# Context matmuls out of the shared two-bank PSUM tile, and its two banks given back one by one

## The chip, the cores and the metric

The kernel runs on one core of a Trainium2 chip. The metric is the device time of one execution in microseconds (us), the median over several runs. Five engines work side by side, each through its own queue in program order: TensorE (PE, matrix products; its weight loads are PEld in the profile), VectorE (DVE), ScalarE (ACT), GpSimd (POOL) and SyncE (SP), which here issues the loads and stores. PSUM, where PE writes its results, has eight banks; a bank takes 512 float32 values on each of the 128 partitions.

## The reference, cut to what matters

Three stages follow one another. The first is chunked attention over 2 x 8 heads, 768 positions and head size 64; the second a mixture of 4 experts without a gate (each expert's result is weighted by normalised probabilities); the third one more pair of products with a leaky activation.

```python
# attention, for each chunk of 32 queries; 8 memory keys, up to 16 keys to the left and 8 to the right
scores = scale * np.matmul(q_c, k_full.transpose(0, 1, 3, 2))
a = np.exp(scores - np.max(scores, axis=-1, keepdims=True))
out[:, :, c_start:c_end] = np.matmul(a / (np.sum(a, axis=-1, keepdims=True) + 1e-09), v_full)
# experts: x is 1536 x 512, w1[e] 512 x 1024, w2[e] 1024 x 512
for e in range(E):
    out += p[:, e:e + 1] * (np.maximum(x @ w1[e], 0.0) @ w2[e])
# last stage: w_in 512 x 2048, w_out 2048 x 512
h = x @ w_in
return (np.maximum(h, 0.0) + alpha * np.minimum(h, 0.0)) @ w_out
```

## The kernel before

**Attention.** The 12 units of 128 queries are cut into 24 half-units (`half_unit`, four heads each). A half-unit has five steps that other work may be put between. Scores: 16 small products, two heads `e` by two pairs of heads `z` by four windows `w` of 32 queries; each takes 64 rows (the head's dimension, so the two `e` use the upper and the lower half of the array) and writes 32 partitions, 64 keys wide. VectorE takes the maximum and subtracts it, ScalarE takes the exponent, two transposes (`t_ps`) put keys on the partitions and ScalarE copies them to `pt`. Context: again 16 small products, 64 rows (the keys of one head) into 32 partitions, 65 wide: 64 values and a column of ones that gives the sum. VectorE adds 1e-9, takes the reciprocal and scales into `xs`; two transposes (`xt_ps`) and a ScalarE copy put the result into `acc`.

Scores and context lie in one PSUM tile, `two`, of two banks (bank `e` for head `e`). Within it the scores of even and odd half-units have columns of their own (`s0`), and the context a third stretch of columns. `load_half` brings a half-unit's queries and keys, `load_v` its values (one transfer, 128 partitions of 2080 bytes in a row) into rings of four half-units (RING, RINGV). Each load is issued by SP behind the products that last read its buffer.

**The order of the work.** The program's order is fixed when it is built, by a model clock `now`: each product adds its planned time (T_S, T_X, T_T, or 13 ns + n/2.4 ns in `mm`), and polls put attention steps, weight preparation (`prep_w`: high and low parts on ScalarE and GpSimd or VectorE) and the conversion of the last stage's weights (`convert`) between the products where the clock says they are due. `Pinned` keeps every engine's instructions in this order. The first 12 half-units run in `att_cycle`: scores of half-unit m, final transposes of m-3, context of m-2, exponent of m, a few filler products (`keep_warm`), transposes of m-1. The other 12 are put between the products of the first tile.

**The products.** The rest is 48 tiles (24 planes of 256 hidden columns by two halves of the columns). `gemm1` is a fast 2x2 block product: seven products a, b, d, a, c, d, c of six matmuls, 384 columns each, in four PSUM banks that VectorE and ScalarE read between them (`add`, `gelu`). `gemm2` is eight results `y` of six matmuls, each read by `evac` when it is complete (VectorE adds it to `acc`). From the third tile on the order is gemm1 of tile k, then gemm2 of tile k-1; only around the change from experts to the last stage (k = 30 to 33) does it differ, since the last stage's input must be complete.

**Banks.** `bank()` hands out PSUM for everything but scores and context. Until the third tile (k = k0 = 2) there are six single banks, tag `ps`. From there on `freed` is set: two of each eight calls get the two halves of a newly allocated two-bank tile, also tagged `two`, and the other six get single banks. A tile takes four calls in gemm1 and eight in gemm2, so the pair falls on d and c of gemm1 in every second tile and on two neighbouring y in every tile. In the profile a product into the pair is named after the call that allocated it, `two_d` (both d and c) or `two_y`.

Almost every instruction of the kernel goes through `Pinned`, and so has line 60; rows are told apart by the tiles' names.

Of the kernel before, what the change touches and what calls it, by code (L numbers as in the profile page):

```python
# [21 lines left out]
WIN = CH  # L22
# [9 lines left out]
P = 128  # L32
# [33 lines left out]
def tile_kernel(ctx: ExitStack, tc: tile.TileContext, qk, v, wa, wq, dpt, alpha, out):  # L66
# [5 lines left out]
    xp = ctx.enter_context(tc.tile_pool(name="xp", bufs=1))  # L72
    bp = ctx.enter_context(tc.tile_pool(name="bp", bufs=1))
    dp = ctx.enter_context(tc.tile_pool(name="dp", bufs=1, space=bass.MemoryType.DRAM))
    ps = ctx.enter_context(tc.tile_pool(name="ps", bufs=1, space=bass.MemoryType.PSUM))
    two = ps.tile([P, 2, 512], F32, tag="two", name="two")
    taken, freed = [0], []

    def bank(name):
        taken[0] += 1  # L80
        if freed and taken[0] % 8 < 2:
            if len(freed) == 1:
                freed.append(ps.tile([P, 2, 512], F32, tag="two", name=f"two_{name}"))
                return freed[1][:, 0]
            return freed.pop()[:, 1]
        return ps.tile([P, 512], F32, tag="ps", bufs=6, name=name)


    ident = cp.tile([P, P], F32, name="ident")
    make_identity(nc, ident)  # L90
# [53 lines left out]
    def keep_warm(hu):  # L144

        o = bank(f"keep{hu}")[:, :NCOL // 2]
        now[0] += 0.1
        for i in range(5 if hu < 6 else 4):
            mm(o, xh[:, 10 + i % 4, NCOL // 2:NCOL // 2 + P], xh[:, 13, spare], n=NCOL // 2, start=True, stop=True)

    def prep_x(c0, n, fast):
# [34 lines left out]
    def mm(*a, n, took=None, **kw):  # L186
        pe_.matmul(*a, **kw)
        now[0] += took or 0.013 + n / 2.4e3


    qk_t = [bp.tile([P, QW + KW], F32, tag="ggB", bufs=4, name=f"qk{i}") for i in range(RING)]
    v_t = [bp.tile([P, 2, NW, VW], F32, tag="w2", bufs=4, name=f"v{i}") for i in range(RINGV // 2)]
    pe_ring = bp.tile([P, 2, HP, 2, KEYS], F32, tag="ft", bufs=3, name="pe_ring")
    pt_ring = bp.tile([P, 2, HP, BLK], F32, tag="fr", name="pt_ring")
    xs_ring = bp.tile([P, 2, HP, 2, D], F32, tag="ft", bufs=3, name="xs_ring")
# [6 lines left out]
    def load_v(hu):  # L202
        if hu >= 2 * NU:
            return
        dst = v_t[hu % RINGV // 2][:, hu % 2].rearrange("p w f -> p (w f)")
        sync.dma_start(dst, v[hu // 2, :, hu % 2])

    def half_unit(u, half):

        hu = 2 * u + half  # L210
        qv = qk_t[hu % RING][:, :QW].rearrange("p (z q) -> p z q", q=BLK)
        kv = qk_t[hu % RING][:, QW:].rearrange("p (z k) -> p z k", k=SPAN)
        vv = v_t[hu % RINGV // 2][:, hu % 2].rearrange("p w (z d) -> p w z d", d=D + 1)
        c, ab = divmod(u, 2)
        cols = slice(c * BLK, (c + 1) * BLK)
        hs = slice(2 * half, 2 * half + 2)
        nm = f"{u}_{half}"

        def tiles():
            now[0] += T_SW  # L220
            for z in range(HP):
                for w in range(NW):
                    for e in range(2):
                        yield z, w, e, slice(w * WIN, (w + 1) * WIN), slice(e * D, (e + 1) * D)

        s0 = hu % 2 * HP * KEYS
        s_ps = two[:, :, s0:s0 + HP * KEYS].rearrange("p e (z k) -> p e z k", k=KEYS)
        for z, w, e, r, rows in tiles():
            mm(s_ps[r, e, z], qv[rows, z, r], kv[rows, z, w * STEP:w * STEP + KEYS], n=KEYS, took=T_S,
               start=True, stop=True)  # L230
        load_half(hu + RING)
        mx = cp.tile([P, 2, HP], F32, tag="mx", bufs=4, name=f"mx{nm}")
        dve.tensor_reduce(out=mx, in_=s_ps, axis=AX.X, op=ALU.max)
        pe = pe_ring[:, hu % 2]
        dve.tensor_tensor(
            out=pe.rearrange("p z e k -> p e z k"), in0=s_ps,
            in1=mx.unsqueeze(3).to_broadcast([P, 2, HP, KEYS]), op=ALU.subtract,
        )
        yield LATE
        act.activation(pe, pe, AF.Exp, scale=scale)  # L240
        yield LAT[0]
        t_ps = bank(f"t{nm}")[:, :HP * BLK].rearrange("p (z q) -> p z q", q=BLK)
        now[0] += T_SW
        for z in range(HP):
            pe_.transpose(t_ps[:, z], pe[:, z].rearrange("p e k -> p (e k)"), ident)
            now[0] += T_T
        pt = pt_ring[:, hu % 2]
        act.copy(pt, t_ps)
        yield LAT[1]
        x_ps = two[:, :, 2 * HP * KEYS:2 * HP * KEYS + VW].rearrange("p e (z d) -> p e z d", d=D + 1)  # L250
        for z, w, e, r, rows in tiles():
            mm(x_ps[r, e, z], pt[rows, z, r], vv[rows, w, z], n=D + 1, took=T_X, start=True, stop=True)
        load_v(hu + RINGV)
        dn = cp.tile([P, 2, HP, 1], F32, tag="dn", bufs=2, name=f"dn{nm}")
        dve.tensor_scalar_add(dn, x_ps[:, :, :, D:D + 1], 1e-9)
        rd = cp.tile([P, 2, HP, 1], F32, tag="rd", bufs=2, name=f"rd{nm}")
        dve.reciprocal(rd, dn)
        xs = xs_ring[:, hu % 2]
        dve.tensor_tensor(out=xs.rearrange("p z e d -> p e z d"), in0=x_ps[:, :, :, :D],
                          in1=rd.to_broadcast([P, 2, HP, D]), op=ALU.mult)  # L260
        yield LAT[2]
        xt_ps = bank(f"xt{nm}")[:, :2 * BLK].rearrange("p (c q) -> p c q", q=BLK)
        now[0] += T_SW
        for z in range(HP):
            pe_.transpose(xt_ps[:, z], xs[:, z].rearrange("p e d -> p (e d)"), ident)
            now[0] += T_T
        act.copy(acc[:, hs, ab, cols], xt_ps)
        if ab == 1 and half == 1:
            while att["x"] < c:
                yield 0.2  # L270
            for _ in prep_x(c * BLK, BLK, c in FAST):
                yield X_STEP[c]
            att["x"] = c + 1
# [339 lines left out]
    def gemm2(p, c0, n, gs, soon, last):  # L613
        prep_force("w", lambda: p in w2)
        wh, wl = w2[p]
        y = {}

        def part(o, ab, i, start, stop, z0=0, z1=n):
            lag_poll(lambda: 2 * i + ab in gs)
            gh, gl = gs[2 * i + ab]  # L620
            if start:
                y[o, ab] = bank(f"y{p}_{c0}_{o}_{ab}_{z0}")[:, :n]
            w_ = [x[:, 2 * i + o // 2, (o % 2) * P:(o % 2 + 1) * P] for x in (wh, wl)]
            for k, (a, b) in enumerate(((w_[0], gh), (w_[1], gh), (w_[0], gl))):
                product(y[o, ab][:, z0:z1], a, b[:, z0:z1], n=z1 - z0,
                        start=start and k == 0, stop=stop and k == 2)
            if stop:
                evac(p, c0 + z0, z1 - z0, o, ab, y[o, ab][:, z0:z1])

        if soon:  # L630

            for o in range(4):
                part(o, 0, 0, True, False)
            for o in range(2):
                part(o, 1, 1, True, False)
            for o in range(4):
                part(o, 0, 1, False, True)
            for o in range(2):
                part(o, 1, 0, False, True)
        else:  # L640
            for o in range(4):
                part(o, 0, 0, True, False)
                part(o, 0, 1, False, True)
            for o in range(2):
                part(o, 1, 1, True, False)
                part(o, 1, 0, False, True)
        for o in range(2, 4):

            end = p == NP - 1 and c0 + n == NCOL and o == 3
            for z0, z1 in ((0, n // 2), (n // 2, n)) if end else ((0, n),):  # L650
                part(o, 1, 1, True, False, z0, z1)
                part(o, 1, 0, False, True, z0, z1)
        if last:
            used2.add(p)
# [27 lines left out]
        order += [(1, k), (2, k - 1)]  # L682
    order += [(2, len(tiles) - 1)]

    for i in range(3):
        load_half(i)
        load_v(i)
    stream("w", weights())
    streams["w"][0] = PREP0
    acts = {}  # L690
    gated = []
    begun = [
        (1, lambda: load_half(3)),
        (1, lambda: load_v(3)),
        (1, lambda: load_raw(0, 0)),
        (2, lambda: sync.dma_start(praw, dpt.rearrange("e (p i) -> p e i", i=NI))),
        (6, lambda: sync.dma_start(nalpha, alpha)),
# [1 line left out]
    for i, (what, k) in enumerate(order):  # L699
        p, c0, n = tiles[k]  # L700
        if k == k0 and what == 1:
            freed.append(None)
            dve.tensor_scalar_mul(nalpha, nalpha, -1.0)
        if what == 1:
            if p == 0:
                while att["done"] < 4 * -(-(c0 + n) // BLK):
# [7 lines left out]
                    if att["done"] >= 3 and not gated:  # L714
                        gated.append(gate())
                        begun.append((11, lambda: load_pb(0, *FIRST[0])))
                        begun.append((12, lambda: load_raw(0, 1)))
            if k == k0:
                stream("c", convert())
                streams["c"][0] = now[0] + 20.0  # L720
# [17 lines left out]

LAT = (1.0, 0.8, 1.6)
LATE = 1.3  # L740
T_S, T_X, T_T, T_SW = 0.016, 0.016, 0.11, 0.1
FAST = (1, 2, 5)
LIVE = 4
PACE = 1.9
PACE0 = 2.0
X_STEP = (1.2, 0.8, 0.4, 1.0, 1.0, 0.4)
PREP0 = 6.0

# [4 lines left out]
T_CONV = 18.0  # L753
DT_X = 0.35
RING = 4
RINGV = 4
WARM = 18


# [72 lines left out]
```

## Time and profile before

| what | value |
|---|---|
| median of 3 runs | 970.69 us (964.85, 970.69, 971.05) |
| the profiled execution's own time | 965.82 us |
| its span, from the first to the last instruction | 964.0 us |
| mean granted TensorE clock, as a share of full speed | 0.985 |

The profile shows one execution. Busy times of engines are unions of their instructions' times; a matmul's start to its end is longer than the distance to the next, because matmuls are pipelined. An idle time is written in brackets behind the instruction that it precedes, with what ended it.

### The profile page before, as it was taken

How to read it: one execution, taken by the hardware profiler on the slowest of the kernel's cores; microseconds unless marked ns; L12 is line 12 of the kernel's file. 1: busy time of each engine (PE TensorE's matmuls, PEld its weight loads, DVE VectorE, ACT ScalarE, POOL GpSimd, SP SyncE). 2: the span in 40 equal slices, each digit the busy share in tenths (PEclk: the TensorE clock that was granted, in tenths of full speed). 3: DMA queues.
4: the chain of work that ended last, by engine and by line, in shares of the span. 5: the costliest groups of instructions: out<-in, count | busy, mean ns of one | idle time of the engine just before them, and what ended most of it. 6: DMA issues, size and time to landing. Idle time of an engine off the chain costs nothing. (4 is left out here: it accounts for less than half of the span.)

```text
span 964.0 us, 15786 instructions
## 1 busy us (share of the span) xinstructions
PE 849.5 (88%) x6046; PEld 798.7 (83%) x6046; DVE 593.4 (62%) x1157; ACT 338.6 (35%) x754; POOL 567.1 (59%) x604
## 2 busy tenths in 40 slices
PE   7778998999998998999998899986789988998997
PEld 5556988988888988888988888886788888888887
DVE  4566556666666666566666566587666556666444
ACT  3555532223223222123222223145355445445341
POOL 2446466766566666566566666565376667654631
PEclk9999999999999999999999999998799999999999
DMA  7762111321221331220331221101021122120103
GB/s 246 236 188 68 45 45 33 115 104 34 77 77 34 106 103 48 73 77 33 98 110 33 88 77 35 53 1 44 22 77 54 58 76 77 55 73 16 55 0 132
DMA packets 28940, 71.76 MB, mean 74 GB/s; under 512 B 4160, under 2 KB 8384, under 8 KB 28864
## 3 DMA queue, kind: packets, MB, share of 16 engines
q1 hardware_dynamic: 28864, 70.75, 22.6%
q8 instruction: 47, 0.77, 0.3%
q14 instruction: 29, 0.24, 0.1%
HBM read 59.18 MB, written 11.56 MB: 73 GB/s over the span
## 5 line engine op out<-in xcount | busy, mean ns | idle before, releaser
L60 PE MATMUL y<-gg,wh 128*128 128x384 f32 x1172 | 317.5, 342 | 8.2 <-ACT gg L60 4.0
L60 POOL TENSOR_TENSOR gg<-g,gg 128x384 fp32r<-128x384 f32 x192 | 197.6, 1034 | 170.6 <-ACT gg L60 156.0
L60 PEld LDWEIGHTS y<-gg,wh 128*128 128x128 f32 x1172 | 216.0, 191 | 11.1 <-ACT gg L60 4.7
L60 PE MATMUL y<-gg,wl 128*128 128x384 f32 x586 | 199.1, 340 | 0.0
L60 DVE TENSOR_TENSOR acc<-y,acc 128x384 f32<-128x384 f32 x265 | 143.2, 552 | 59.1 <-PE y L60 58.1
L60 ACT CAST gg<-g 128x384 fp32r<-128x384 f32 x192 | 97.7, 511 | 194.5 <-DVE g L60 194.0
L60 POOL TENSOR_TENSOR wl<-raw,wh 128x256 fp32r<-128x256 f32 (+1 forms) x115 | 114.7, 1006 | 82.4 <-PE b L60 57.0
L60 PE MATMUL two_y<-gg,wh 128*128 128x384 f32 (+1 forms) x368 | 116.0, 356 | 48.0 <-DVE acc L60 48.0
L60 PEld LDWEIGHTS two_y<-gg,wh 128*128 128x128 f32 x368 | 69.2, 191 | 62.8 <-DVE acc L60 62.8
L60 ACT COPY u<-a 128x384 f32<-128x384 f32 x48 | 23.0, 478 | 270.1 <-PE a L60 270.0
L60 PEld LDWEIGHTS y<-gg,wl 128*128 128x128 f32 x586 | 111.9, 191 | 0.0
L60 PE MATMUL two_d<-xh,wh 128*128 128x384 f32 x184 | 67.3, 366 | 31.3 <-DVE b L60 16.0
L60 DVE TENSOR_TENSOR acc<-two_y,acc 128x384 f32<-128x384 f32 x88 | 48.6, 552 | 66.0 <-PE two_y L60 65.7
L60 POOL TENSOR_TENSOR wl<-s,wh 128x256 fp32r<-128x256 f32 x92 | 69.0, 757 | 16.8 <-ACT wh L60 16.6
L60 PEld LDWEIGHTS two_d<-xh,wh 128*128 128x128 f32 x184 | 34.7, 189 | 46.5 <-DVE b L60 23.3
L60 PE MATMUL a<-xh,wh 128*128 128x384 f32 x192 | 65.4, 340 | 0.5 <-ACT u L60 0.5
L60 DVE TENSOR_TENSOR u<-b,u 128x384 f32<-128x384 f32 x48 | 26.7, 557 | 62.1 <-PE b L60 57.2
L60 PE MATMUL a<-xh,wl 128*128 128x384 f32 x192 | 64.9, 338 | 0.0
L60 PE MATMUL a<-xl,wh 128*128 128x384 f32 x192 | 64.9, 338 | 0.0
L60 POOL TENSOR_TENSOR fl<-fl,fm 128x512 f32<-128x512 f32 x32 | 41.2, 1287 | 38.8 <-issue 24.2
L60 PE MATMUL two_y<-gg,wl 128*128 128x384 f32 (+1 forms) x184 | 62.8, 341 | 0.0
L60 PE MATMUL two_d<-xh,wl 128*128 128x384 f32 x184 | 62.5, 340 | 0.0
(113 smaller groups left out, 1663.8 us busy)
## 6 DMA issues: line engine op xcount, KB each, us to landing
raw<-in_wa SPq DMA_DIRECT2D x32, 512.0 KB, 3.8
fr<-in_wq SPq DMA_DIRECT2D x32, 512.0 KB, 3.8
w2s<-fl SPq DMA_DIRECT2D x32, 256.0 KB, 2.3
raw<-w2s SPq DMA_DIRECT2D x16, 512.0 KB, 3.8
qk<-in_qk SPq DMA_DIRECT2D x24, 312.0 KB, 3.7
v<-in_v SPq DMA_DIRECT2D x24, 260.0 KB, 3.5
pb<-p_dram SPq DMA_DIRECT2D x8, 384.0 KB, 3.4
outT<-acc SPq DMA_DIRECT2D x15, 192.0 KB, 1.9
```

Source lines behind the costliest of these rows:

```text
L60: return self.tc.keep_in_program_order(f(*a, **kw))
```

## The change

Scores keep the two-bank tile, which now comes from a pool of its own (`sc`); all scores lie at column 0, without separate columns for even and odd half-units. The context of a half-unit gets a single bank of the ring: eight products instead of 16, each with 128 rows (the keys of both heads `e`) against a block-diagonal value tile, 130 wide. The value tile has zeros where head and rows don't match; they are set once, by four memsets. The values arrive in two transfers of 64 partitions for each half-unit, each partition's 2080 bytes scattered in eight runs of 260, and the ring of values has two half-units instead of four. When attention is over (before gemm1 of k = 1, one tile earlier than before), the pool of scores is closed and a pool of two single banks (`pm`) takes its place; every fourth call of `bank` goes there. The first two tiles' gemm2 (p = 0) gets another order of its parts, with fewer results open at a time. Some planned times change, and `keep_warm` has 5 filler products for the first three half-units instead of the first six.

```diff
-    ps = ctx.enter_context(tc.tile_pool(name="ps", bufs=1, space=bass.MemoryType.PSUM))
-    two = ps.tile([P, 2, 512], F32, tag="two", name="two")
-    taken, freed = [0], []
+    ps = ctx.enter_context(tc.tile_pool(name="ps", bufs=6, space=bass.MemoryType.PSUM))
+    scores = ExitStack()
+    two = scores.enter_context(tc.tile_pool(name="sc", bufs=1, space=bass.MemoryType.PSUM)).tile(
+        [P, 2, 512], F32, tag="two", name="two")
+    taken, more = [0], []
     def bank(name):
         taken[0] += 1
-        if freed and taken[0] % 8 < 2:
-            if len(freed) == 1:
-                freed.append(ps.tile([P, 2, 512], F32, tag="two", name=f"two_{name}"))
-                return freed[1][:, 0]
-            return freed.pop()[:, 1]
-        return ps.tile([P, 512], F32, tag="ps", bufs=6, name=name)
+        if more and taken[0] % 4 == 0:
+            return more[0].tile([P, 512], F32, tag="pm", name=name)
+        return ps.tile([P, 512], F32, tag="ps", name=name)
+    def attention_over():
+        scores.close()
+        more.append(ctx.enter_context(tc.tile_pool(name="pm", bufs=2, space=bass.MemoryType.PSUM)))
...
-        for i in range(5 if hu < 6 else 4):
+        for i in range(5 if hu < 3 else 4):
...
-    v_t = [bp.tile([P, 2, NW, VW], F32, tag="w2", bufs=4, name=f"v{i}") for i in range(RINGV // 2)]
+    v_t = [bp.tile([P, HP, NW, 2, D + 1], F32, tag="w2", bufs=4, name=f"v{i}") for i in range(RINGV)]
+    for vt in v_t:
+        for e in range(2):
+            (pool, dve)[e].memset(vt[(1 - e) * D:(2 - e) * D, :, :, e], 0.0)
...
-        dst = v_t[hu % RINGV // 2][:, hu % 2].rearrange("p w f -> p (w f)")
-        sync.dma_start(dst, v[hu // 2, :, hu % 2])
+        for e in range(2):
+            rows = slice(e * D, (e + 1) * D)
+            sync.dma_start(v_t[hu % RINGV][rows, :, :, e].rearrange("p z w d -> p (z w) d"),
+                           v[hu // 2, rows, hu % 2].rearrange("p (a d) -> p a d", d=D + 1))
...
-        s0 = hu % 2 * HP * KEYS
-        s_ps = two[:, :, s0:s0 + HP * KEYS].rearrange("p e (z k) -> p e z k", k=KEYS)
+        s_ps = two[:, :, :HP * KEYS].rearrange("p e (z k) -> p e z k", k=KEYS)
...
-        x_ps = two[:, :, 2 * HP * KEYS:2 * HP * KEYS + VW].rearrange("p e (z d) -> p e z d", d=D + 1)
-        for z, w, e, r, rows in tiles():
-            mm(x_ps[r, e, z], pt[rows, z, r], vv[rows, w, z], n=D + 1, took=T_X, start=True, stop=True)
+        x_ps = bank(f"x{nm}")[:, :2 * VW].rearrange("p (z e d) -> p z e d", e=2, d=D + 1)
+        for z in range(HP):
+            for w in range(NW):
+                mm(x_ps[win[w], z].rearrange("p e d -> p (e d)"), pt[:, z, win[w]], vv[:, z, w], n=2 * (D + 1),
+                   took=T_X, start=True, stop=True)
...
         if k == k0 and what == 1:
-            freed.append(None)
...
+            if k == k0 - 1:
+                attention_over()
...
-T_S, T_X, T_T, T_SW = 0.016, 0.016, 0.11, 0.1
+T_S, T_X, T_T, T_SW = 0.017, 0.06, 0.11, 0.1
-PACE0 = 2.0
+PACE0 = 2.2
-RINGV = 4
+RINGV = 2
```

## Rows read from the trace of the kernel before

**Rows 1.** Page, part 1: busy time, share of the span and instructions of each engine.

```profile
PE 849.5 (88%) x6046; PEld 798.7 (83%) x6046; DVE 593.4 (62%) x1157; ACT 338.6 (35%) x754; POOL 567.1 (59%) x604
```

**Rows 2.** PE's waits, whole span: tile waiting, released by; us in total, times, longest.

```profile
PE two_y L60 <- DVE acc L60: 48.0, 46, 4.4
PE two_d L60 <- DVE b L60: 16.0, 23, 1.4
PE two_d L60 <- DVE two_d L60: 15.1, 23, 0.7
```

**Rows 3.** PE's timeline, two waits: start, us, instruction, [idle before <- what ended it].

```profile
243.48 0.34 PE L60 MATMUL two_y<-gg,wh 128*128 128x384 f32 x1
244.47 0.45 PE L60 MATMUL two_y<-gg,wh 128*128 128x384 f32 x1 [0.65 <-DVE acc L60]
...
268.89 0.45 PE L60 MATMUL two_d<-xh,wh 128*128 128x384 f32 x1 [0.66 <-DVE b L60]
```

**Rows 4.** VectorE's timeline, at the start, in attention and in the product phase.

```profile
5.73 0.42 DVE L60 TENSOR_REDUCE mx<-two 128x4 f32<-128x256 f32 x1 [4.79 <-PE two L60]
...
16.64 0.42 DVE L60 TENSOR_TENSOR pe_ring<-two,mx 128x256 f32<-128x256 f32 x1
...
243.86 0.56 DVE L60 TENSOR_TENSOR acc<-two_y,acc 128x384 f32<-128x384 f32 x1 [0.49 <-PE two_y L60]
```

**Rows 5.** Chain that ended last, in order of time: start, us, what.

```profile
810.56 1.04 PE a L60 x6
...
833.77 6.28 PE y L60 x36
...
959.65 0.68 PE y L60 x6
```

**Rows 6.** ScalarE's timeline: the copy behind each gemm1's first product, four of 48.

```profile
122.66 0.47 ACT L60 COPY u<-a 128x384 f32<-128x384 f32 x1
...
607.23 0.48 ACT L60 COPY u<-a 128x384 f32<-128x384 f32 x1 [5.99 <-PE a L60]
...
700.13 0.46 ACT L60 COPY u<-a 128x384 f32<-128x384 f32 x1
...
933.23 0.48 ACT L60 COPY u<-a 128x384 f32<-128x384 f32 x1 [6.39 <-PE a L60]
```

**Rows 7.** Windows: us, busy (instructions) by engine, then granted clock, DMA share, GB/s.

```profile
113.00:632.00 519.00, 474.07 (x2612) 455.79 (x2611) 324.32 (x607) 134.36 (x299) 328.97 (x348) 0.99 0.21 68
632.00:700.00 68.00, 52.78 (x243) 47.87 (x241) 50.21 (x80) 30.38 (x64) 36.90 (x37) 0.85 0.07 24
```

**Rows 8.** PE's timeline, one cycle of the first 12 half-units.

```profile
17.17 0.46 PE L60 MATMUL two<-v,pt_ring 64*32 64x65 f32 x32 [0.82 <-ACT acc L60]
17.56 1.15 PE L60 MATMUL keep<-xh 128*128 128x384 f32 x5
...
18.87 0.46 PE L60 MATMUL two<-qk 64*32 64x64 f32 x32
19.25 0.44 PE L60 MATMUL xt<-ident,xs_ring 128*128 128x128 f32 x2
20.50 0.46 PE L60 MATMUL two<-v,pt_ring 64*32 64x65 f32 x32 [0.81 <-ACT acc L60]
```

**Rows 9.** Groups by form: context and scores; busy us, mean ns | idle before, releasers.

```profile
L60 PE MATMUL two<-v,pt_ring 64*32 64x65 f32 x768 | 11.5, 223 | 15.1 <-ACT acc L60 6.7 <-issue 3.8 <-ACT xh L60 2.6
L60 PE MATMUL two<-qk 64*32 64x64 f32 x768 | 11.2, 226 | 5.2 <-DVE xs_ring L60 5.0
```

**Rows 10.** Windows around one weight load and one 48-byte store; landing of the values' loads.

```profile
102.50:104.75 2.25, 2.25 (x15) 2.25 (x14) 2.15 (x4) 0.97 (x2) 0.61 (x2) 1.00 0.71 240
23.95:24.52 0.57, 0.44 (x33) 0.38 (x33) 0.03 (x1) 0.42 (x1) 0.57 (x2) 1.00 0.59 44
...
DMA to landing us min/median/max: 2.7/3.5/6.0
```

**Rows 11.** VectorE's waits, whole span: one of them.

```profile
DVE g L60 <- POOL gg L60: 12.2, 22, 1.4
```

More of the change, by code (lines that the diff above doesn't have):

```diff
@@ L212, in half_unit @@
         kv = qk_t[hu % RING][:, QW:].rearrange("p (z k) -> p z k", k=SPAN)
-        vv = v_t[hu % RINGV // 2][:, hu % 2].rearrange("p w (z d) -> p w z d", d=D + 1)
+        vv = v_t[hu % RINGV].rearrange("p z w e d -> p z w (e d)")
         c, ab = divmod(u, 2)
@@ L217, in half_unit @@
         nm = f"{u}_{half}"
[L219 to L224, printed above, removed]
-        s0 = hu % 2 * HP * KEYS
-        s_ps = two[:, :, s0:s0 + HP * KEYS].rearrange("p e (z k) -> p e z k", k=KEYS)
-        for z, w, e, r, rows in tiles():
-            mm(s_ps[r, e, z], qv[rows, z, r], kv[rows, z, w * STEP:w * STEP + KEYS], n=KEYS, took=T_S,
-               start=True, stop=True)
+        win = [slice(w * WIN, (w + 1) * WIN) for w in range(NW)]
+        s_ps = two[:, :, :HP * KEYS].rearrange("p e (z k) -> p e z k", k=KEYS)
+        now[0] += T_SW
+        for z in range(HP):
+            for w in range(NW):
+                for e in range(2):
+                    rows = slice(e * D, (e + 1) * D)
+                    mm(s_ps[win[w], e, z], qv[rows, z, win[w]], kv[rows, z, w * STEP:w * STEP + KEYS], n=KEYS,
+                       took=T_S, start=True, stop=True)
         load_half(hu + RING)
@@ L249, in half_unit @@
         yield LAT[1]
-        x_ps = two[:, :, 2 * HP * KEYS:2 * HP * KEYS + VW].rearrange("p e (z d) -> p e z d", d=D + 1)
-        for z, w, e, r, rows in tiles():
-            mm(x_ps[r, e, z], pt[rows, z, r], vv[rows, w, z], n=D + 1, took=T_X, start=True, stop=True)
+        x_ps = bank(f"x{nm}")[:, :2 * VW].rearrange("p (z e d) -> p z e d", e=2, d=D + 1)
+        now[0] += T_SW
+        for z in range(HP):
+            for w in range(NW):
+                mm(x_ps[win[w], z].rearrange("p e d -> p (e d)"), pt[:, z, win[w]], vv[:, z, w], n=2 * (D + 1),
+                   took=T_X, start=True, stop=True)
         load_v(hu + RINGV)
-        dn = cp.tile([P, 2, HP, 1], F32, tag="dn", bufs=2, name=f"dn{nm}")
+        dn = cp.tile([P, HP, 2, 1], F32, tag="dn", bufs=2, name=f"dn{nm}")
         dve.tensor_scalar_add(dn, x_ps[:, :, :, D:D + 1], 1e-9)
-        rd = cp.tile([P, 2, HP, 1], F32, tag="rd", bufs=2, name=f"rd{nm}")
+        rd = cp.tile([P, HP, 2, 1], F32, tag="rd", bufs=2, name=f"rd{nm}")
         dve.reciprocal(rd, dn)
         xs = xs_ring[:, hu % 2]
-        dve.tensor_tensor(out=xs.rearrange("p z e d -> p e z d"), in0=x_ps[:, :, :, :D],
-                          in1=rd.to_broadcast([P, 2, HP, D]), op=ALU.mult)
+        dve.tensor_tensor(out=xs, in0=x_ps[:, :, :, :D], in1=rd.to_broadcast([P, HP, 2, D]), op=ALU.mult)
         yield LAT[2]
@@ L628, in part @@
                 evac(p, c0 + z0, z1 - z0, o, ab, y[o, ab][:, z0:z1])
-        if soon:
+        if p == 0:
+            for o in range(2):
+                part(o, 0, 0, True, False)
+            for o in range(4):
+                part(o, 1, 1, True, False)
+                part(o, 1, 0, False, True)
+            for o in range(2):
+                part(o, 0, 1, False, True)
+            for o in range(2, 4):
+                part(o, 0, 0, True, False)
+                part(o, 0, 1, False, True)
+        elif soon:
             for o in range(4):
@@ L646, in gemm2 @@
                 part(o, 1, 0, False, True)
-        for o in range(2, 4):
+        for o in range(2, 4) if p else ():
             end = p == NP - 1 and c0 + n == NCOL and o == 3
@@ L683, in tile_kernel @@
     order += [(2, len(tiles) - 1)]
-    for i in range(3):
+    for i in range(2):
         load_half(i)
         load_v(i)
+    load_half(2)
     stream("w", weights())
@@ L693, in tile_kernel @@
         (1, lambda: load_half(3)),
-        (1, lambda: load_v(3)),
         (1, lambda: load_raw(0, 0)),
@@ L798 @@
     qk = np.concatenate([halves(qs, BLK), halves(ks, SPAN)], axis=3)
-    vs = vs.reshape(NU, KEYS, 2, HP, 2, NW, D + 1).transpose(0, 4, 1, 2, 5, 3, 6)
+    vs = vs.reshape(NU, KEYS, 2, HP, 2, NW, D + 1).transpose(0, 4, 1, 2, 3, 5, 6)
     def pairs(wi, wo):
```

## The prediction

> **What bounds the kernel now.** I read the page's busy shares first: PE 849.5 of 964.0 us, no other engine above 62% [rows 1]. So the end is set by PE, and what can be gained is its idle time of about 114 us, or work taken from it. Next, PE's waits by releaser: three lines, all in front of a product into the two-bank tile, make 48.0 + 16.0 + 15.1 = 79.1 us in 46 + 23 + 23 = 92 waits [rows 2]. The six single banks have no line of that size. The timelines show what such a wait is. A product into the second half of the pair could follow its forerunner (start 243.48) at once, but starts at 244.47 [rows 3], 0.05 us after VectorE has finished reading the *first* half (243.86 + 0.56 = 244.42, [rows 4]). In gemm1 the second d product starts only when VectorE has read c, which lies in the other bank (268.89, [rows 3]). So the pair is guarded as one tile: PE waits for a reader of a bank that it isn't writing.
>
> On this the Trainium skill, PSUM — Partial Sum Buffer, section "PSUM bank collisions raise a hardware error", says that two engines in different banks run clean, and only the same bank and quadrant must be kept apart. By that rule the wait isn't asked for by the chip and goes with the pair; if the chip did ask for it, single banks would change nothing.
>
> What a wait costs is more than its idle time. Stall-free, seven products of gemm1 take 1.04 us each and 36 matmuls of y take 6.28 us, 0.174 each [rows 5]. From 243.48 to 244.47 are 0.99 us, 0.82 more than 0.17, and the first matmul after it is 0.11 longer than others (0.45 against 0.34, [rows 3]): 0.93 us lost where the row says 0.65. So 79.1 us of idle time stand for about 79.1 + 92 x 0.28 = 105 us.
>
> **The change part by part.**
>
> *The pair becomes two single banks.* I cross-check the 105 us by tile periods. A stall-free tile is 7 x 1.04 + 48 x 6.28 / 36 = 15.65 us [rows 5]. The copies behind gemm1's first product mark the tiles [rows 6]. Between 122.66 and 607.23 lie 27 tiles: 484.57 us against 27 x 15.65 = 422.6, so 62.0 us lost. Between 700.13 and 933.23 lie 13: 233.1 against 203.5, so 29.6 lost. The last gemm1's first product begins some 1.1 us before its copy, at 932.1; gemm1 and two gemm2 make 7.28 + 2 x 8.37 = 24.0 us, to 956.1, while the last y ends at 960.33 [rows 5]: 4.2 lost. These 95.8 us are nearly all waits of the pair, and go.
>
> Between 607.23 and 700.13 lie four tiles (62.6 us) in 92.9 us: 30.3 lost. Here the last stage's input is prepared; VectorE is busy 50.2 of 68 us, the clock granted is 0.85, part of it at the lower level of 1.2 GHz behind the stalls [rows 7], and PE truly depends on VectorE, ScalarE and GpSimd. Even the longest wait of the pair (4.4 us, [rows 2]) lies here, and behind it VectorE is simply late. I let 8 of the 30 go (bounds 3 and 15).
>
> What is late next? VectorE has 324.3 us of work in 519, GpSimd 329.0 [rows 7]; per tile (519 / 17.95 = 28.9 tiles) that is 11.2 and 11.4 us, 73% of 15.65. Neither becomes the bound on average, but they wait for each other in order: VectorE's gelu waits for GpSimd 12.2 us in all [rows 11], and a late VectorE frees banks late. With eight banks, four held by gemm1, PE can run four products (4.2 us) ahead of the reader. I charge 5 us for new waits (bounds 0 and 25).
>
> *Context in a bank of the ring, scores alone in the pair.* In attention the same whole-tile guard works between scores and context. In a cycle of the first half-units PE could start the context when its forerunners are done, but starts at 17.17 [rows 8], just behind VectorE's read of the next half-unit's scores (16.64 + 0.42 = 17.06, [rows 4]). The cycle is 20.50 - 17.17 = 3.33 us: context 0.39, fillers and transposes 1.31, scores 0.38, transposes 0.44, wait 0.81. Over all 24 half-units 15.1 us stand idle before context and 5.2 before scores [rows 9]. A part has other reasons (`pt` not ready); I take 12 of 20 us as removed (bounds 5 and 20). Scores lose their second set of columns, but the next scores come a cycle later, long after VectorE has read them, and the guard already made them wait: nothing.
>
> Context itself: eight products of 128 rows and 130 columns instead of 16 of 64 rows and 65 columns. The same columns pass, but on four tiles of the array side by side instead of eight: 0.39 us as now at the low end, 0.78 at the high end. I take 0.6, nearer to the high end since columns decide once the products are few: 24 x 0.2 = 5 us (0 to 9). Readers see the same sizes. Three half-units with one filler less: 3 x 0.2 = 0.6 us, left out.
>
> *Loads of the values.* For each half-unit 1024 packets of 260 bytes instead of 128 of 2080. A load of 128 packets of 4096 bytes keeps the 16 engines 0.71 x 2.25 us busy, 200 ns a packet; 512 packets of 48 bytes take 0.59 x 0.57 us, 10 ns a packet [rows 10]. On the line between, 260 bytes cost 20 ns and 2080 bytes 105: 1.3 us instead of 0.8 for a half-unit, beside 1.0 for queries and keys. That fits into a cycle of 2.7 us. The values land in 3.5 us, at most 6.0 [rows 10]; 0.5 more for the data and as much, a guess, for the second transfer issued behind the first make 4.5, at most 7.0. With two buffers instead of four the load is issued two cycles ahead, 5.4 us minus the context: just enough, late sometimes. I charge 2 us (0 to 25; the upper end is a rival below). SP's queue behind it holds the next queries and keys, two cycles from use.
>
> *Four memsets* stand before the first value loads on SP's queue. VectorE and PE wait for the first loads until 5.73 anyway [rows 4]; 1 us (0 to 2). *Rest:* attention gives 12 - 5 - 2 - 1 = 4 us back. The new order for p = 0, the earlier release by one tile and the planned times move work without adding any; nothing, since that tile runs from six banks now and no wait of its banks is large [rows 2].
>
> *Sum,* against the profiled execution's own 965.8 us (964.0 of span and 1.8 around it): -95.8 - 8 + 5 - 4 = -102.8, so 863. The median of the three runs lies 4.9 us above that execution; the waits that go are probably part of that spread, so I add 2 and not 4.9: **865 us**.
>
> **The rivals.**
>
> *Half the gain is taken by VectorE and GpSimd.* For it: 73% load on two in-order queues, and already now the waits before `two_y` average 48.0 / 46 = 1.04 us [rows 2] where a bare one is 0.65 [rows 3]: VectorE was late. Against it: single banks of the same tiles hardly wait today. If each of the 46 tiles with a pair kept 1.1 of its 2.1 us: 865 + 50 = 915.
>
> *Attention is held up by the value loads.* If a 260-byte packet costs 40 ns, twice the line, a half-unit needs 2.6 + 1.0 = 3.6 us of transfer against a cycle of 2.7: 24 x 0.9 = 22 us, 887. The Trainium skill, DMA: Bandwidth & Descriptors, section "Specifications", asks for at least 512 bytes per packet for full rate and so speaks against these runs. Against it here: 48-byte packets at 10 ns [rows 10], though those were stores.
>
> *The change doesn't do what it says:* the wait for VectorE has another cause than the shared tile and stays. Nothing in the timelines speaks for it; 96 of the 103 us would be missing: 961.
>
> *Slower:* value packets cost by number, not by bytes. At the 200 ns of a 4096-byte packet [rows 10] a half-unit takes 1024 x 0.2 / 16 = 12.8 us, plus 1.0; 24 x (13.8 - 2.7) = 266 us, so 865 + 266 = 1131. It decides from (970.7 - 865) / 24 = 4.4 us a half-unit, that is 7.1 us of transfer, 95 ns a packet: about what the line gives for 2080 bytes. The 10 ns of a 48-byte packet speak against it.
>
> **How the numbers follow.** Pure gain 0.66 (own range 846 to 885), value loads 0.13 (875 to 900), half the gain 0.14 (895 to 935), no effect 0.04 (955 to 972), slower 0.03. The range goes from 846 to 912, which leaves out the last two, half of the half gain and a little below. A measurement of this kernel tells about 1% from no change. Faster by over 1% (below 961): 0.66 + 0.13 + 0.14 + 0.01 = 0.94; within 1%: 0.03; slower: 0.03.
>
> **What would show it.** Right: no PE waits for VectorE in front of products into another bank; tile periods of 15.7 to 15.9 us; PE's share of the span above 93%; the changeover from experts to last stage still some 20 us longer than its work; context products 0.5 to 0.8 us a half-unit; cycles of about 2.7 us in the first half-units. Wrong: periods of 16.5 and more with waits for VectorE or GpSimd in front of y or c; context waiting for values in attention; cycles of 3.3 us or longer.

## The result: 859.6 us, a ratio of 0.887

| | before | after |
|---|---|---|
| median of the runs, us | 970.36 (964.85 to 971.05, 4 runs) | 859.62 (859.42 to 861.38, 4 runs) |
| ratio, 95% interval | | 0.8874 [0.8839, 0.8908] |
| profiled execution, us; its span | 965.8; 964.0 | 859.42; 857.6 |
| forecast | | 865 (846 to 912) |

A second set of runs, shown with the experiments (after_again), gave 0.8863 [0.8839, 0.8888]. The forecast case, pure gain, is what came.

The page of the changed kernel, part 1 (busy us, share of the span, instructions), answers [rows 1]:

```profile
PE 827.4 (96%) x5659; PEld 801.5 (93%) x5659; DVE 593.8 (69%) x1159; ACT 337.7 (39%) x754; POOL 575.3 (67%) x606
```

VectorE's work is the same to 0.4 us; PE's idle time fell from 114.5 us to 30.2. PE is also busy for 22 us less than before, with the same large products. Most of that fits what a wait adds beside its idle time: the product in front of it counts as busy for 0.17 us that otherwise overlap with the next one, and the product behind it is 0.11 us longer (both worked out in the prediction from [rows 3] and [rows 5]); 92 x 0.28 = 26 us.

PE's waits over the whole span, the longest five lines (tile, released by; us, times, longest), answer [rows 2]:

```profile
PE x L60 <- DMA v<-in_v: 10.9, 9, 2.8
PE y L60 <- POOL gg L60: 4.4, 6, 1.4
PE y L60 <- ACT gg L60: 2.7, 3, 1.6
PE two L60 <- DMA qk<-in_qk: 2.4, 2, 1.6
PE c L60 <- DVE b L60: 1.7, 2, 0.9
```

The waits in front of products into the pair are gone, and no line has taken their place in the products. Between 120 and 560 us the same view lists no wait of PE at all; the y and c lines lie in the changeover (the tiles around the change from experts to last stage), at 577 to 612, all but 0.8 us. New, and first, stands a wait of attention: the context product `x` for the values' loads.

ScalarE's timeline, the same four copies as in [rows 6] (start, us, instruction, idle before):

```profile
124.86 0.47 ACT L60 COPY u<-a 128x384 f32<-128x384 f32 x1
...
547.46 0.48 ACT L60 COPY u<-a 128x384 f32<-128x384 f32 x1 [5.49 <-PE a L60]
...
628.41 0.46 ACT L60 COPY u<-a 128x384 f32<-128x384 f32 x1
...
831.17 0.48 ACT L60 COPY u<-a 128x384 f32<-128x384 f32 x1 [4.89 <-PE a L60]
```

They cut the run into five stretches, and the 106.4 us of span saved into five parts:

| stretch | before | after | gained | forecast |
|---|---|---|---|---|
| up to the first copy (attention) | 122.66 | 124.86 | -2.2 | 4 |
| 27 tiles | 484.57 | 422.60 | 62.0 | 62.0 |
| changeover, 4 tiles | 92.90 | 80.95 | 12.0 | 8, less 5 for new waits anywhere |
| 13 tiles | 233.10 | 202.76 | 30.3 | 29.6 |
| last gemm1 to the end | 30.77 | 26.43 | 4.3 | 4.2 |

The first row compares one execution with one. Four profiled executions with the changed attention and its loads (this one, its repeat, the second and the third experiment) opened the 27 tiles between 123.42 and 125.78 us.

Windows of the changed kernel (us, busy time and instructions of PE, PEld, DVE, ACT, POOL, then granted clock, DMA share, GB/s), to be read beside [rows 7]:

```profile
100.00:560.00 460.00, 459.25 (x2635) 458.49 (x2634) 327.83 (x614) 142.28 (x316) 338.21 (x355) 1.00 0.24 79
560.00:620.00 60.00, 51.52 (x250) 48.03 (x249) 50.45 (x81) 24.78 (x52) 35.84 (x34) 0.89 0.08 27
620.00:857.00 237.00, 234.50 (x1348) 233.83 (x1346) 156.98 (x301) 122.47 (x264) 153.91 (x162) 1.00 0.20 68
0.00:97.00 97.00, 79.10 (x1415) 58.15 (x1416) 56.82 (x162) 45.62 (x118) 47.30 (x56) 0.93 0.84 183
```

In the two long product stretches PE is busy for 459.25 of 460 and 234.5 of 237 us. What is left to gain lies in the first 97 us (18 idle, and the granted clock at 0.93 where the kernel before had 1.00) and in the changeover (8.5 idle, clock 0.89).

PE's timeline in attention, early half-units and two late contexts, beside [rows 8]:

```profile
13.43 0.65 PE L60 MATMUL x<-v,pt_ring 128*32 128x130 f32 x16
14.01 0.97 PE L60 MATMUL keep<-xh 128*128 128x384 f32 x4
...
15.12 0.71 PE L60 MATMUL two<-qk 64*32 64x64 f32 x32
...
17.97 1.09 PE L60 MATMUL x<-v,pt_ring 128*32 128x130 f32 x16 [1.77 <-DMA v<-in_v]
18.99 1.65 PE L60 MATMUL keep<-xh 128*128 128x384 f32 x4
...
21.84 0.65 PE L60 MATMUL x<-v,pt_ring 128*32 128x130 f32 x16
22.42 0.96 PE L60 MATMUL keep<-xh 128*128 128x384 f32 x4
...
24.28 0.65 PE L60 MATMUL x<-v,pt_ring 128*32 128x130 f32 x16
...
76.17 1.09 PE L60 MATMUL x<-v,pt_ring 128*32 128x130 f32 x16 [2.79 <-DMA v<-in_v]
```

Context takes 0.58 us (13.43 to 14.01), and a cycle that waits for nothing takes 24.28 - 21.84 = 2.44 us, with four fillers, where [rows 8] had 3.33 with five. But the context at 17.97 waited 1.77 us for its values, and behind that wait the same 16 instructions and the four fillers took 1.09 and 1.65 us instead of 0.65 and 0.97: the granted clock was 0.50 (windows in the last section). The loads themselves, by tile (issue time in ns on SP's queue, min/median/max, first and last start) and by landing, beside [rows 10]:

```profile
L60 SPq DMA_DIRECT2D v<-in_v x48: 595/596/1385, 1.2 to 85.7; - x48
...
DMA to landing us min/median/max: 3.2/4.6/7.7
```

### The profile page after: what moved, and what is told of

Same layout as the page of the kernel before. It is cut to its first block, busy times and chain, and to the rows that moved or that the text cites. A ratio compares the mean times of both kernels' runs of the same rounds, so it can differ in the third digit from the quotient of the medians.

```text
span 857.6 us, 15042 instructions
## 1 busy us (share of the span) xinstructions
PE 827.4 (96%) x5659; PEld 801.5 (93%) x5659; DVE 593.8 (69%) x1159; ACT 337.7 (39%) x754; POOL 575.3 (67%) x606
## 4 chain that ended last, share of the span: by engine, by line
PE 85%; DMA 5%; DVE 4%; issue 2%; ACT 1%; SPq 1%; POOL 1%; POOLq 0%; DVEq 0%; ACTq 0%
PE y L60 45%; PE c L60 11%; PE a L60 11%; PE d L60 11%; PE b L60 5%; DMA v<-in_v 4%; DVE st L60 2%; PE x L60 1%; SPq L60 1%; DVE xl L60 1%; PE keep L60 1%; DMA qk<-in_qk 1%; ACT xh L60 1%; POOL gg L60 1%; DVE acc L60 1%
## 5 line engine op out<-in xcount | busy, mean ns | idle before, releaser
L60 PE MATMUL y<-gg,wh 128*128 128x384 f32 x1540 | 407.3, 341 | 7.1 <-POOL gg L60 4.4
L60 PEld LDWEIGHTS y<-gg,wh 128*128 128x128 f32 x1540 | 282.0, 190 | 11.0 <-POOL gg L60 6.8
L60 PE MATMUL y<-gg,wl 128*128 128x384 f32 (+1 forms) x770 | 260.6, 338 | 0.0
L60 PE MATMUL c<-xh,wh 128*128 128x384 f32 x192 | 64.7, 337 | 1.7 <-DVE b L60 1.7
L60 PE MATMUL c<-xh,wl 128*128 128x384 f32 x192 | 65.1, 339 | 0.0
L60 PE MATMUL d<-xh,wh 128*128 128x384 f32 x192 | 64.5, 336 | 0.4 <-DVE t L60 0.4
L60 PE MATMUL d<-xl,wh 128*128 128x384 f32 x192 | 64.1, 334 | 0.4 <-issue 0.4
L60 PE MATMUL c<-xl,wh 128*128 128x384 f32 x192 | 64.4, 335 | 0.0
L60 PE MATMUL d<-xh,wl 128*128 128x384 f32 x192 | 64.2, 334 | 0.0
L60 ACT CAST wh<-raw 128x256 fp32r<-128x256 f32 (+1 forms) x120 | 55.9, 489 | 0.6 <-PE a L60 0.6
```

The costliest lines, as they stand in the source:

```text
L60: return self.tc.keep_in_program_order(f(*a, **kw))
```

## The experiments

The theory before the first run: nearly all of the gain is the whole-tile guard of the pair and goes with the pair, not with the rest of the change; attention's share is about nothing, because late values take back what the smaller guard gives. The rivals: that attention brings part of the gain; that the gain comes from how the banks are spread over the calls (every fourth call instead of two neighbours); and, for the values, that the number of short runs delays them, against the two buffers. Each short diff is against the changed kernel and cut to the lines that matter (... marks a cut).

**The bank scheme alone.** Attention, its loads, the order of the first two tiles' gemm2 and the planned times are those of the kernel before; only the banks are those of the change, with the pool of scores closed one tile later, where the kernel before gave the pair back. Of the bank part, only this differs from the changed kernel:

```diff
         if k == k0 and what == 1:
+            attention_over()
...
-            if k == k0 - 1:
-                attention_over()
```

> The kernel before with the bank part alone: scores and context stay in the shared two-bank tile, which is given back as two single banks behind the second tile; loads, memsets and the order of the first two tiles as before. Theory (the whole gain is the guard of the pair, and the attention part costs about 2 us): 964.0 - 106.4 - 2 = about 856 us of span, 857 to 859 us of time, tile periods of 15.7 us, no wait of PE for VectorE in front of another bank. Rival (the split of context, the earlier release or the new order of the first tiles is needed too): over 880 us.

Measured: 861.8 us (858.49 to 863.17), ratio 0.8908 [0.8859, 0.8956]. PE's waits, the first four lines:

```profile
PE two L60 <- ACT acc L60: 6.7, 9, 0.8
PE two L60 <- DVE xs_ring L60: 5.0, 5, 1.6
PE y L60 <- POOL gg L60: 4.6, 5, 1.4
PE two L60 <- issue: 4.3, 6, 1.8
```

The guard waits that remain belong to attention (`two`); those of `two_y` and `two_d` are gone, and the tile periods are those of the changed kernel (15.64 to 15.84 us behind first ones of 14.82 and 14.45). The time is 3 us above the expected 857 to 859. 2.8 us lie in attention, where the granted clock fell after a wait that the kernel before has too, there without a fall (rows in the last section). The interval overlaps the changed kernel's: the bank scheme by itself brings all of the gain that can be measured, and the rival that needs the rest of the change (over 880 us) falls.

**The attention part alone.** The changed kernel, but from the third tile on the two banks are handed out as a two-bank tile again, as before.

```diff
-        if more and taken[0] % 4 == 0:
-            return more[0].tile([P, 512], F32, tag="pm", name=name)
+        if len(more) > 1 and taken[0] % 8 < 2:
+            if len(more) == 2:
+                more.append(more[0].tile([P, 2, 512], F32, tag="pm", name=f"two_{name}"))
+                return more[2][:, 0]
+            return more.pop()[:, 1]
...
-        more.append(ctx.enter_context(tc.tile_pool(name="pm", bufs=2, space=bass.MemoryType.PSUM)))
+        more.append(ctx.enter_context(tc.tile_pool(name="pm", bufs=1, space=bass.MemoryType.PSUM)))
...
         if k == k0 and what == 1:
+            more.append(None)
```

> The changed kernel with the pair put back: from the third tile on two of each eight calls get the halves of a two-bank tile, as before; attention as changed. Theory: the waits before products into the pair are back, about 79 us in 92 waits, tile periods of 17.9 us; 857.6 + 106.4 + 2 = about 966 us of span, 966 to 973 us of time. Rival (the attention part brings a share of the gain by itself): under 950 us.

Measured: 967.2 us (962.92 to 970.31, 10 runs), ratio 0.9987 [0.9955, 1.0019]. PE's waits, the first four lines:

```profile
PE two_y L60 <- DVE acc L60: 48.0, 46, 4.4
PE two_d L60 <- DVE b L60: 16.0, 23, 1.4
PE two_d L60 <- DVE two_d L60: 15.2, 23, 0.7
PE x L60 <- DMA v<-in_v: 12.7, 10, 3.0
```

The first three lines are [rows 2] again, to 0.1 us, and the time is the old one: the span of the profiled execution is 962.6 us, 105.0 more than the changed kernel's. Banks alone give 0.891, the rest alone 0.999, whose interval leaves it at most 4.4 us: the gain is the banks'.

**Single banks, neighbouring calls.** The two banks stay single ones, but two neighbouring calls of eight get them, as the pair did.

```diff
-        if more and taken[0] % 4 == 0:
+        if more and taken[0] % 8 < 2:
```

> The changed kernel, with the two single banks handed out at the same two neighbouring calls of eight that the pair had. Theory (PE waited because the two banks were guarded as one tile): as the changed kernel, 858 to 863 us, no waits for VectorE of 0.6 us before y or d and c. Rival (it waited because two neighbouring calls share two banks that come free late): waits stay, at least 30 us of them, over 890 us.

Measured: 860.27 us (859.33 to 860.81), ratio 0.8896 [0.8843, 0.8948]. PE's waits for VectorE in front of c and d, all in the changeover, and one tile in PE's and VectorE's timelines, beside [rows 3]:

```profile
PE c L60 <- DVE b L60: 1.7, 2, 0.9
PE d L60 <- DVE t L60: 1.1, 1, 1.1
```
```profile
301.39 0.33 PE L60 MATMUL d<-xh,wh 128*128 128x384 f32 x1
...
301.59 0.57 DVE L60 TENSOR_TENSOR b<-c,t 128x384 f32<-128x384 f32 x1 [0.41 <-PE c L60]
```

The same calls as in the pair, in the same order, without the shared tile: the second d product starts before VectorE begins to read c, where in the pair it waited for the end of that read. No wait for VectorE is left outside attention and the changeover. What cost the time was one tile over two banks, not the order in which the banks come round.

**One load of the values.** The value tile with its zeros is laid out in DRAM, so one transfer of 128 partitions with 4160 bytes each takes the place of the two; no memsets; still two buffers, and twice the bytes.

```diff
-        for e in range(2):
-            rows = slice(e * D, (e + 1) * D)
-            sync.dma_start(v_t[hu % RINGV][rows, :, :, e].rearrange("p z w d -> p (z w) d"),
-                           v[hu // 2, rows, hu % 2].rearrange("p (a d) -> p a d", d=D + 1))
+        sync.dma_start(v_t[hu % RINGV].rearrange("p z w e d -> p (z w e d)"), v[hu // 2, :, hu % 2])
...
```

> The changed kernel, with the block-diagonal value tile laid out with its zeros in memory, so that a half-unit's values come in one transfer of 128 runs of 4160 bytes instead of two with 1024 runs of 260; no memsets; still two buffers. Twice the bytes. Theory (the values are late because of the many short runs and the long issue on SP, 1.28 us for the two): waits of PE for values fall from 10.9 to under 3 us, the granted clock of the first 90 us goes from 0.92 to nearly 1, 844 to 850 us. Rival (two buffers are too few for any load, whatever its form): waits stay at 8 us and more, 856 to 862 us; with doubled bytes perhaps more.

Measured: 855.46 us (853.32 to 856.93), ratio 0.8845 [0.8800, 0.8891]. The wait, and the issue time of the loads:

```profile
PE x L60 <- DMA v<-in_v: 7.9, 8, 2.5
```
```profile
L60 SPq DMA_DIRECT2D v<-in_v x24: 327/328/745, 1.2 to 77.1; - x24
```

The waits are 7.9 us, where the changed kernel had 10.9 and its repeat 8.7: they stay, and the theory's "under 3" was wrong. The time lies between the theory's range and the rival's, and by its interval it is not told apart from the changed kernel's. So the run decides nothing about the runs of 260 bytes, the less so as it moves twice the bytes; it shows that two loads instead of one are not the main cause.

**Long runs.** The value tile with the head first, so each of the two transfers writes 64 runs of 2080 bytes instead of 512 of 260.

```diff
-    v_t = [bp.tile([P, HP, NW, 2, D + 1], F32, tag="w2", bufs=4, name=f"v{i}") for i in range(RINGV)]
+    v_t = [bp.tile([P, 2, HP, NW, D + 1], F32, tag="w2", bufs=4, name=f"v{i}") for i in range(RINGV)]
...
-            sync.dma_start(v_t[hu % RINGV][rows, :, :, e].rearrange("p z w d -> p (z w) d"),
-                           v[hu // 2, rows, hu % 2].rearrange("p (a d) -> p a d", d=D + 1))
+            sync.dma_start(v_t[hu % RINGV][rows, e].rearrange("p z w d -> p (z w d)"), v[hu // 2, rows, hu % 2])
...
```

> The changed kernel with the value tile ordered head first, so that each of the two transfers of a half-unit writes 64 runs of 2080 bytes instead of 512 of 260; same bytes, same zeros, same two buffers; the product reads two stretches of 65 columns. Theory (number of runs): the issue on SP falls from 0.6 to 0.3 us a transfer, values land in 3.5 to 4 us instead of 4.6, PE waits for values under 4 us instead of 10.9, 845 to 852 us. Rival (two buffers are too few): waits of 7 us and more, 854 to 860 us.

Measured: 853.32 us (851.82 to 857.61), ratio 0.8860 [0.8833, 0.8887]. The wait, and the loads:

```profile
PE x L60 <- DMA v<-in_v: 8.4, 6, 2.9
```
```profile
L60 SPq DMA_DIRECT2D v<-in_v x48: 465/544/1127, 1.2 to 81.2; - x48
...
DMA to landing us min/median/max: 2.5/3.8/7.9
```

The loads land 0.8 us earlier in the median, but the latest as late as before, and by the ratio the time is not told apart from the changed kernel's 0.8874 and 0.8863. The median of 853.3 us lies between the theory's range and the rival's; the waits, 8.4 us, are the rival's (7 and more). The theory of the number of runs falls; two buffers for a load that can take 7.9 us stand. The expected issue time of 0.3 us was wrong as well: it came out at 0.54.

**No late values.** The changed kernel without the loads after the first two: all half-units use the values of the first two, so the attention it computes is that of other values.

```diff
-        load_v(hu + RINGV)
```

> The changed kernel without the value loads behind the first two half-units; the later ones use the values of the first two (this part of the computation is changed). It measures what late values cost in all. Theory (10.9 us of waits, and some 5 us of products at the lower clock behind three of them): 842 to 847 us, granted clock of the first 97 us near 1. Rival (the waits only stand in the place of others, for queries and keys or ScalarE): 852 us and more.

Measured: 844.33 us (844.12 to 846.21), ratio 0.8762 [0.8735, 0.8790]. The window of attention, and the copy that opens the 27 tiles:

```profile
0.00:97.00 97.00, 89.00 (x1496) 68.94 (x1497) 68.80 (x180) 54.69 (x137) 54.23 (x64) 1.00 0.46 133
```
```profile
109.42 0.47 ACT L60 COPY u<-a 128x384 f32<-128x384 f32 x1
```

The copy comes 124.86 - 109.42 = 15.4 us earlier, of which 10.9 are the waits themselves; the granted clock is 1.00 over the stretch instead of 0.93, which is where the other 4.5 fit. By the ratios, each against the kernel before in its own round, it is (0.8874 - 0.8762) x 965 = 10.8 us. So late values cost the changed kernel 11 to 15 us. Part of this could be the traffic that is left out with the loads; the next kernel has this traffic and is no slower by its ratio (its copy stands at 113.63).

**Four buffers in the first half.** Long runs as above, and four value buffers for the first 12 half-units; two of them are given back before the product phase needs their space, and the other 12 half-units have two.

```diff
...
+    def ring(hu):
+        return 4 if hu < 12 else 2
...
-        load_v(hu + RINGV)
+        if hu not in (10, 11):
+            load_v(hu + ring(hu))
...
```

> As the kernel with long runs, and four value buffers for the first 12 half-units (the two further ones are given back before the first tile's second weights need their room); the other 12 keep two. Theory (two buffers leave a load only two cycles, some 5 us, and a load that meets a weight load takes up to 8): no wait for values in the first 12 half-units, where the kernel with long runs has 6.6 of its 8.4 us, and no fall of the clock there; 844 to 850 us. Rival (the loads are late because the queues are full, not because they are issued late): waits of 5 us and more stay, 851 to 857 us.

Measured: 847.79 us (846.33 to 848.74), ratio 0.8744 [0.8724, 0.8763]. Waits and window:

```profile
PE x L60 <- DMA v<-in_v: 0.2, 1, 0.2
```
```profile
0.00:97.00 97.00, 86.76 (x1475) 66.34 (x1476) 68.33 (x180) 52.89 (x133) 51.22 (x61) 0.98 0.69 189
```

**The changed kernel again,** on the same chip, unedited.

> The changed kernel once more, beside the one with four buffers: 859 to 862 us.

Measured: 858.47 us (856.84 to 861.99), ratio 0.8863 [0.8839, 0.8888]. The intervals of this ratio and of the one with four buffers are apart; 10.7 us lie between the medians.

With four buffers the loads land no sooner after their issue (4.3 us in the median and 7.6 at most, against 3.8 and 7.9 with long runs and two buffers); they are only issued two half-units sooner, and the waits, 8.4 us there, are gone (also in the half-units that keep two buffers, where 1.8 us became 0.2). That is the cause of the late values: two buffers. By the intervals this kernel beats the changed one and the one with long runs (0.8860). One expected thing did not come: the granted clock did fall once, after a wait of 1.74 us in front of the scores at 16.76. Four buffers with the runs of 260 bytes were not tried, nor four for all half-units.

## Why the prediction was right

**The pair.** The step that carried the sum, 95.8 us in the 40 tiles and the end, came out at 62.0 + 30.3 + 4.3 = 96.6. The tile periods, 15.64 to 15.81 us behind a first one of 14.80 and 14.45 in the two stretches, are the stall-free 15.65 that was worked out from [rows 5]; that 62.0 came out to the tenth is luck, since the short first period makes up for some 0.03 us more in each other. That the price of a wait is its idle time and the restart, 79.1 + 92 x 0.28 = 105 us, is borne out by the second experiment: the same waits, 79.2 us of idle time, and 105.0 us of span. The rule that the Trainium skill gives in PSUM — Partial Sum Buffer, section "PSUM bank collisions raise a hardware error", that two engines in different banks run clean, agrees with the traces: with single banks in the same order (third experiment) PE writes d from 301.39 while VectorE reads c from 301.59 to 302.16, and no wait for VectorE is left in these tiles.

**New waits, 5 us.** In the product stretches there are none outside the changeover; the rival in which VectorE and GpSimd take half of the gain did not come, although their load rose to 327.83 and 338.21 us of 460, 71 and 74%. Two queues loaded by three quarters did not make PE wait, with eight banks to run ahead in.

**The changeover.** 12.0 us gained where 8 were let go; it is still 80.95 - 62.6 = 18.3 us longer than its work, as the "some 20" said. The 8 and the 5 for new waits were mis-sized to the same side: together 9 us too little gain. Both lie inside their stated bounds (3 to 15, and 0 to 25).

**Attention.** Here the sum of 4 us came out at -2.2 (-0.8 to -3.1 by the four executions), two of its terms were wrong in size, and a sign that the prediction had listed under "wrong" came: context waiting for values. The step "The values land in 3.5 us [...] just enough, late sometimes. I charge 2 us" failed: landing came as forecast (4.6 and 7.7 at most, forecast 4.5 and 7.0), but the charge was sized by the middle of these times, and it had no term for the clock. With two half-units ahead instead of four, the values of nine half-units of 24 came too late, with waits of up to 2.8 us and, behind the longer ones, slow products: 11 to 15 us, inside the stated bounds of 0 to 25, between the charge and the rival's 22. The rival's own reason, packets twice as dear, was not it: with long runs the time stayed, and in the changed kernel's trace the 24576 packets of 260 bytes took 26 ns each in the mean and 19 in the median, where the line gave 20 and the rival 40. The other term was too small on the good side: without late values the first copy came at 109.42, 13.2 us before the kernel before, where guard, context and memsets together had been put at 12 - 5 - 1 = 6; with four buffers, and so with the loads, it came at 113.63, 9.0 before. Its parts agree where a row shows them: context 0.58 us (0.6 forecast) and an undisturbed cycle of 2.44 (2.7 forecast, with one filler of 0.2 us more). That the cycle's wait was the guard for VectorE's read of the scores was argued from two times, while [rows 8] names ScalarE's copy to `acc` as the releaser. In the changed kernel such a cycle has no wait for either; no run took the guard away by itself.

**Short runs.** In the stretch from 30 to 60 us the DMA engines were 1.01 busy at 212 GB/s with runs of 260 bytes, and 0.78 at 218 GB/s with runs of 2080 in the kernel with long runs (0.72 at 216 before). The windows of the first two:

```profile
30.00:60.00 30.00, 23.07 (x476) 16.38 (x481) 18.22 (x52) 15.13 (x40) 10.80 (x11) 0.94 1.01 212
```
```profile
30.00:60.00 30.00, 23.87 (x460) 16.70 (x437) 18.61 (x52) 15.03 (x40) 11.07 (x12) 0.89 0.78 218
```

So the short runs cost the DMA engines time. By the trace's packets a half-unit's values took 1024 x 26 ns / 16 = 1.7 us of the 16 engines, against 0.9 before (107 ns in the mean for one of 2080 bytes); the forecast had 1.3 and 0.8. The Trainium skill, DMA: Bandwidth & Descriptors, section "Specifications", which wants at least 512 bytes for full rate, agrees with that; the time of the kernel, which the same exchange did not change by its ratio, was not bound by it.

**The sum.** -96.6 - 12.0 + 2.2 = -106.4 us of span against a forecast of -102.8: errors of 9 us for the better in changeover and new waits, of 6 for the worse in attention, the rest in the pair. That they partly cancel is luck. The 2 us that were added for the spread of the median were not needed: 859.62 us against 859.42 of the profiled execution.

## What to carry to other kernels

Where a tile spans several banks and independent products share it, look at the wait's releaser: if it reads another bank than the one being written, single-bank tiles remove the wait without moving any work, and the gain is the idle time plus the slower restart of each wait, which the tile period shows. When a ring of buffers is cut, compare the *longest* landing of its loads, not the median, with the cycles that the ring is ahead; here four buffers for the first 12 half-units, with longer runs, were worth 10.7 us, while merging or lengthening the transfers was worth nothing that could be told.

## What the runs showed of the hardware

**Behind some waits of 1.6 to 2.8 us the granted clock was halved, behind others not.** Windows of the changed kernel in attention (the granted clock is the third number from the end):

```profile
14.00:18.00 4.00, 2.23 (x48) 1.60 (x45) 1.76 (x6) 1.58 (x4) 2.03 (x3) 0.98 1.23 205
18.00:20.00 2.00, 2.00 (x19) 1.61 (x20) 0.77 (x3) 0.00 (x0) 0.00 (x0) 0.50 0.85 178
22.00:24.00 2.00, 2.00 (x55) 1.50 (x48) 1.72 (x9) 1.05 (x3) 0.74 (x1) 1.00 0.72 182
50.00:52.00 2.00, 2.00 (x38) 1.52 (x37) 0.42 (x1) 0.33 (x1) 0.00 (x0) 0.50 1.16 213
78.00:80.00 2.00, 2.00 (x37) 1.26 (x35) 1.02 (x4) 1.07 (x3) 0.74 (x1) 0.50 0.58 101
```

Behind the waits of 1.77, 1.99 and 2.79 us (contexts at 17.97, 48.50 and 76.17) the granted clock was 0.50, the level of 1.2 GHz, while PE was busy all the time; at 22 it was back at 2.4 GHz. Behind the waits of 1.63 and 1.41 us (7.76 and 28.22) it stayed at 1.00. In the kernel with four buffers one wait of 1.74 us, in front of the scores at 16.76, was followed by 0.50. This is where the time fits that 10.9 us of waiting cost beyond 10.9.

The length of a wait alone does not decide it. The kernel with the bank scheme alone has the attention of the kernel before, and both wait 1.57 us in front of a scores product (58.38 and 58.06). The windows behind it, first the bank scheme alone, then the kernel before:

```profile
60.00:66.00 6.00, 6.00 (x110) 4.61 (x110) 1.61 (x5) 3.04 (x9) 2.19 (x4) 0.50 0.49 151
```
```profile
60.00:66.00 6.00, 4.92 (x130) 3.95 (x118) 3.23 (x11) 4.03 (x11) 4.27 (x6) 1.00 0.65 186
```

The next scores product that waits starts at 67.29 and 64.46: a distance of 0.3 us has become 2.8, and the 27 tiles open 2.8 us later (125.48 against 122.66). The kernel before kept 1.00 behind a wait of 1.79 us too (context at 44.15), and in the repeat of the changed kernel a wait of 1.69 us (47.61) was followed by 0.50 and one of 1.86 (75.77) was not. What decides is open.

**Issuing a transfer has a price that goes with its shape.** A load of 64 partitions held SP's queue for 0.54 us (runs of 2080 bytes) or 0.60 (260 bytes), one of 128 partitions for 0.33, with 2080 (kernel before, below) or with 4160 bytes in each. Two half loads therefore cost the queue more than three times what one whole load does. Why is open.

```profile
L60 SPq DMA_DIRECT2D v<-in_v x24: 327/328/433, 1.2 to 74.4; - x24
```
